# One transposition in place of two for the sinks' weights in a fused sink-attention and feed-forward kernel

## The chip, the cores and the metric

The kernel runs on one core of a Trainium2 chip. The metric is the device time of one execution in microseconds (us), as the median of three runs. One execution was taken by the hardware profiler; all rows below come from that one.

## The reference

Attention with a sliding window and sinks, then a feed-forward block on its output:

```python
B, H, S, D = 4, 8, 768, 64              # float32 all through
keep = (pos_k < n_sink) | ((rel >= 0) & (rel < window))     # n_sink 4, window 128
a = softmax(where(keep, q @ k.T / sqrt(D), -1e9))
x = (a @ v)  as [B*S = 3072, H*D = 512]
h = x @ w_in                            # 512 x 2048
g = h * erf(softplus(h))
out = g @ w_out                         # 2048 x 512
```

## The kernel before

**Steps and units.** The attention is cut into 48 steps. Step `s` takes 256 queries of two heads: `g, c = divmod(s, 4)` gives a block of 256 rows and a pair of heads; three blocks make one batch. The feed-forward block is cut into 192 units (12 row blocks of 256 by 16 slices of the hidden width), and four units go with one step. The position of a step on the planner's time axis is `pos(s)`, 54 for step 15 and four more for each next step; a unit is one position.

**A step's parts** have one-letter names in the plan: `q` and `v` load (SyncE's queue), `p` (`prep`) transposes q and k into the PSUM tile `tqk`, `s` (`score`) makes the scores `ps`, `f` (`soft`) masks them on VectorE and takes exponents on ScalarE into `pst`, `n` (`norm`) divides by the sums, `t` (`ptrans`) transposes the window's weights into `tp`, `w` (`sinkw`) and `u` (`strans`) deal with the sinks' weights, `a` (`av`) multiplies with v, `x` (`xfin`) splits the result into a high and a low part. `H`, `A`, `P` and `R` are the feed-forward block: first product, activation, second product and result. `k` (`sinks`) prepares the sinks' rows of v once per batch.

**The sinks' weights.** `pst` holds 144 columns for each of four quarters (two tiles of queries `i` by two heads `h`): 128 for the window and 16 for the sinks. `sinkw` splits the sinks' columns on VectorE into rounded, rest and rounded again (two copies and a subtraction into `sh`), `strans` transposes `sh` twice, once for each tile of queries, into the PSUM tile `ts`, and one ScalarE copy makes `sp` from it. `av` multiplies `sp` (128 rows: rounded, rest, rounded, zeros) by `sv`, whose rows are v's rounded part twice, v's rest, and zeros.

**Buffers.** `tqk`, `tp`, `ts` and `av` share the two PSUM buffers of the tag `t`. A buffer is free for the next tile when the last reader of its tile is done. `sp` has two buffers, `pst` a ring of two.

**What sets the order.** Every part is emitted with a priority worked out from its place on the time axis (`at`), and a planner orders each engine's instructions by its own costs and those priorities. The first steps follow lists written out by hand. From the position `fixed = pos(NF1) - 0.5` on, TensorE's instructions are chained in the order of the plan; VectorE, ScalarE and GpSimd stay with the planner. Between the lists and `fixed` the planner orders TensorE too. The plan's rows for a step differ on the two sides of `NF1`: in the free part the scores and `av` come at `a + 0.14`, the transpositions at `a + 2.15`; in the fixed part at `a - 0.3` and `a + 3.01`, with loads and `prep` earlier.

Of the kernel before, what the change touches and what calls it, by code (L numbers as in the profile page):

```python
# [9 lines left out]
F32 = mybir.dt.float32  # L10
BF16 = mybir.dt.bfloat16
F32R = mybir.dt.float32r
I32 = mybir.dt.int32
AF = mybir.ActivationFunctionType
ALU = mybir.AluOpType
# [4 lines left out]
P = 128  # L20
SW = 16
# [18 lines left out]
LO = 4.5  # L40

NE, AL = 4, 2
NF1 = 16

PW, EA = 256, 40
O = dict(prep=-100, norm=-100, core=-300, av=-300, load=-400, ptrans=-200, xfin=-100,
# [21 lines left out]
def kernel(  # L68
# [11 lines left out]
    nc = tc.nc  # L80
# [3 lines left out]
    NPAIR = H // 2  # L84
# [3 lines left out]
    GPB = S // GT  # L88
    NG = B * GPB
    NU = 4  # L90
    NSTEP = NG * NPAIR
    KB = P + SW
    scale = 1.0 / math.sqrt(D)
# [5 lines left out]
    ident = cpool.tile([P, P], F32, name="ident")  # L99
# [36 lines left out]
    def fast_path():  # L136
        with ExitStack() as st:
            pers = st.enter_context(tc.tile_pool(name="pers", bufs=1))
            raw = st.enter_context(tc.tile_pool(name="raw", bufs=2))
            qkp = st.enter_context(tc.tile_pool(name="qkp", bufs=1))  # L140
            work = st.enter_context(tc.tile_pool(name="work", bufs=2))
# [14 lines left out]
                out=kw[:, :256], in0=rf[:, :256], scalar=0.0, in1=kw[:, :256], op0=ALU.is_ge, op1=ALU.mult  # L156
# [28 lines left out]
            sv = pers.tile([P, NPAIR, P], F32R, name="sv")  # L185
            nc.gpsimd.memset(sv.bitcast(F32), 0.0)

            pst = pers.tile([P, RING, 2, 2, KB], F32, name="pst")

            shs = [pers.tile([P, 7, 2 * SW], F32R, name=f"sh{i}") for i in range(2)]  # L190
            for x in shs:
                nc.gpsimd.memset(x[:, 6].bitcast(F32), 0.0)
            pers.tile([P, 32], F32, name="gap")
            xp = {}

            stp, tail = {}, {}
# [44 lines left out]
            vec, ten, syn = (Line(x) for x in (nc.vector, nc.tensor, nc.sync))  # L241
# [25 lines left out]
            def sinks(s):  # L267

                g, c = divmod(s, NPAIR)
                d = stp[s]  # L270
                if g % GPB == 0:
                    for r0 in (0, 32):
                        (nc.gpsimd.tensor_copy if s < NE else nc.scalar.copy)(sv[r0 : r0 + 32, c, :], d["sv"])
                    vec.tensor_tensor(sv[64:96, c, :], d["sv"], sv[:32, c, :].bitcast(F32), op=ALU.subtract)

            dx = KB + 80
            X = [80, 80 + dx]
# [38 lines left out]
            def soft(s):  # L316
# [26 lines left out]
                if gb < GPB - 1:  # L343
                    syn.dma_start(kq[:, c, 0, :P], kq[:, c, 2, :P])

            def norm(s):
                d = stp[s]
                sm = d["sum"]
                vec.tensor_scalar_add(sm, sm, 1.0e-9)
                fill()  # L350
                vec.reciprocal(sm, sm)
                fill()
                for i in range(2):
                    for h in range(2):
                        p = d["pst"][:, i, h, :]
                        if 4 <= s < 8:
                            nc.scalar.activation(p, p, AF.Copy, scale=sm[:, i, h : h + 1])
                        else:
                            vec.tensor_scalar_mul(p, p, sm[:, i, h : h + 1])
# [20 lines left out]
            def sinkw(s):  # L380

                d = stp[s]
                sh = shs[s % 2][:, :6].rearrange("p (i r) t -> p i r t", i=2)
                x = d["pst"][:, :, :, P:]
                for r in (0, 2):
                    vec.tensor_copy(sh[:, :, r].rearrange("p i (h t) -> p i h t", h=2), x)
                vec.tensor_tensor(
                    sh[:, :, 1].rearrange("p i (h t) -> p i h t", h=2), x,
                    sh[:, :, 0].rearrange("p i (h t) -> p i h t", h=2).bitcast(F32), op=ALU.subtract,
                )  # L390
            def strans(s):

                d = stp[s]
                pool, tag = (ps_o, "o") if s < 6 else (ps_t, "t")
                ts = pool.tile([P, 2, P], F32, tag=tag, name=f"ts_{s}")
                for i in range(2):
                    x = shs[s % 2][:, 3 * i : 3 * i + 4].rearrange("p r t -> p (r t)").bitcast(F32)
                    ten.transpose(out=ts[:, i, :], in_=x, identity=ident)
                sp = d["sp"] = work.tile([P, 2, P], F32R, tag="sp", bufs=AL, name=f"sp_{s}")
                nc.scalar.copy(sp, ts)  # L400
# [44 lines left out]
            def pos(s):  # L445

                return 3 * s if s < NE else 4 * s - 4 * NE + 3 * NE - 2
# [34 lines left out]
            def fill():  # L482

                for w in list(todo):
                    try:
                        next(w)
                    except StopIteration:
                        todo.remove(w)
# [24 lines left out]
            def add(a, nm, j):  # L513
                ev.append((a, len(ev), nm, j))
# [23 lines left out]
            def use(n):  # L538
# [3 lines left out]
            order = sorted(range(32), key=use)  # L542
            acts = {
                "q": ("load", loadqk), "v": ("load", loadv), "p": ("prep", prep), "k": ("prep", sinks), "s": ("core", score),
                "f": ("core", soft), "n": ("norm", norm), "t": ("ptrans", ptrans), "w": ("ptrans", sinkw), "u": ("ptrans", strans),
                "a": ("av", av), "x": ("xfin", xfin), "H": ("hid", hid), "A": ("act", act), "P": ("proj", proj), "R": ("res", res),
                "L": ("wl", lambda j: wload(order[j])), "C": ("wc", lambda j: todo.append(wconv(order[j], j))), "D": ("wc", drain),
# [6 lines left out]
            def needs(nm, j):  # L554

                pin = [("C", order.index(n)) for n in range(j // NC * NC, j // NC * NC + NC)] if nm == "H" else []
                return {
                    "p": [("q", j), ("f", j - NPAIR)],
                    "s": [("p", j), ("f", j - 1 if j != 3 else 0)] if j > 1 else [("p", j)],
                    "f": [("s", j), ("t", j - (4 if j < 6 else 2)), ("w", j - (4 if j < 6 else 2))],  # L560
                    "n": [("f", j)],
                    "t": [("n", j), ("a", j - AL)],
                    "w": [("n", j), ("u", j - 2)],
                    "u": [("w", j), ("t", j)],
                    "k": [("v", j), ("p", j)],
                    "a": [("u", j), ("v", j)] + [("k", j)] * (j < NE),
                    "x": [("a", j)],
                    "H": pin + [("x", 3), ("f", 2), ("H", j - 1)] + [("A", j - 3)] * (j % 2 == 0),
                    "A": [("H", j), ("P", j - 4)],
                    "P": [("A", j | 1), ("C", order.index(16 + j if j < 16 else 0)), ("u", 5)],  # L570
                    "q": [("p", j - 2)],
                    "v": [("a", j - 3)],
                    "C": [("L", j)],
                    "L": [("C", j - WQ)],
                }.get(nm, [])
# [3 lines left out]
            done, a = set(), LEAD - 10  # L579
            while any(lines):  # L580
                before = len(done)
                for x in lines:
                    while x and all(w in done for w in needs(*x[0]) if w in known):
                        w = x.pop(0)
                        a = LEAD + w[1] if w[0] == "H" else a + 0.012
# [4 lines left out]

            fixed = pos(NF1) - 0.5
            for s in range(NE, NSTEP + AL):
                a = pos(s)
                if s < NF1:
                    plan = (
                        ("a", a + 0.139, s - AL), ("x", a + 1.11, s - AL), ("n", a + 1.12, s), ("p", a - 2.87, s), ("k", a - 2.869, s),
                        ("s", a + 0.14, s), ("f", a + 0.141, s), ("t", a + 2.15, s), ("w", a + 2.151, s), ("u", a + 2.152, s),
                        ("q", a - 3.84, s), ("v", a - 3.839, s),
                    )
                else:  # L600
                    plan = (
                        ("a", a - 0.3, s - AL), ("s", a - 0.29, s), ("f", a - 0.289, s), ("x", a - 0.285, s - AL), ("n", a + 1.12, s),
                        ("w", a + 2.151, s), ("t", a + 3.01, s), ("u", a + 3.02, s),
                        ("q", a - (8.2 if s > NF1 + 1 else 6.5 - 2 * (s - NF1)), s), ("p", a - (4.28 if s > NF1 else 2.87), s),
                        ("k", a - 2.869, s), ("v", a - 3.839, s),
                    )
                for nm, z, n in plan:
                    if NE <= n < NSTEP and (nm, n) not in done and (nm != "k" or n // NPAIR % GPB == 0):
                        add(max(z, last + 0.01) if nm in "ntwu" else z, nm, n)
            for m in range(NG * NF):  # L610
                g, f = divmod(m, NF)
                a = m + LEAD
                p = LAG + 0.3
                if a + p > fixed:
                    p = LAG + (1.0 if m % 2 == 0 else 0.0) + (0.01 if m % 4 > 1 else 0.03) + 0.005 * (m % 2)
# [80 lines left out]
    def general_path():  # L696

        NT_S = S // P
        with ExitStack() as st:
# [71 lines left out]
            with tc.tile_pool(name="g_one1", bufs=1) as one, tc.tile_pool(name="g_work1", bufs=2) as work:  # L771
# [3 lines left out]
                with tc.For_i(0, B, 1) as b:  # L775
                    for gb in range(GPB):
# [25 lines left out]
                        for i in range(2):  # L802
# [3 lines left out]
                            )  # L806

    fast_path()
    ok = nc.values_load(flagi[0:1, 0:1], min_val=0, max_val=1)
    with tc.If(ok == 0):  # L810
# [31 lines left out]
```

## Time and profile before

| | |
|---|---|
| median of three runs | 749.41 us (748.31 to 750.84) |
| the profiled execution | 750.56 us, of which the span from first to last instruction is 748.8 us |
| granted TensorE clock, mean | 0.994 |
| TensorE busy | 713.3 us, 95% of the span |
| VectorE busy | 506.2 us, 68% |
| ScalarE busy | 534.2 us, 71% |
| GpSimd busy | 185.7 us, 25% |

How to read it: PE is TensorE's matmul row, PEld its weight loads, DVE VectorE, ACT ScalarE, POOL GpSimd, SP SyncE. A busy time is the union of the instructions' recorded stretches; matmuls overlap each other in the record, so that the distance from one start to the next, and not the duration, says how much of TensorE one takes.

### The profile page before, as it was taken

What the parts mean: (1) busy time and instruction counts of PE and PEld (TensorE: products, weight loads), DVE (VectorE), ACT (ScalarE), POOL (GpSimd) and SP (SyncE); (2) the same over time, 40 slices, a digit from 0 to 9 for tenths busy, and PEclk for the clock granted to TensorE, in tenths of its full rate; (3) what the DMA queues carried; (4) which work ended last, traced back from release to release, by engine and by line L of the source; (5) the groups of instructions that cost most, each with busy time, mean ns of one, the idle gap of its engine ahead of it and who ended that gap; (6) DMA issues with size and microseconds to landing.
All of it is one profiled execution on the core that took longest, in us unless ns stands there. A gap on an engine that the chain in (4) does not pass through costs nothing. (4 is left out here: it accounts for less than half of the span.)

```text
span 748.8 us, 14851 instructions
## 1 busy us (share of the span) xinstructions
PE 713.3 (95%) x5168; PEld 593.3 (79%) x5168; DVE 506.2 (68%) x1493; ACT 534.2 (71%) x1265; POOL 185.7 (25%) x220
## 2 busy tenths in 40 slices
PE   4888999899999999999999999999999999999996
PEld 2564666677788888888888888888888888888995
DVE  7899999897776566576566666556667566563442
ACT  3576769776786867778677777777787776775663
POOL 2220001222322322332232232232232232232221
PEclk9899999999999999999999999999999999999999
DMA  5687541111121121111111211112112211000000
GB/s 143 186 251 273 200 148 43 34 29 37 54 58 29 57 54 26 54 34 40 54 44 43 57 39 41 54 24 50 46 38 54 61 29 36 29 13 1 29 1 32
DMA packets 100595, 47.33 MB, mean 63 GB/s; under 512 B 89248, under 2 KB 93344, under 8 KB 100512
## 3 DMA queue, kind: packets, MB, share of 16 engines
q1 hardware_dynamic: 99680, 46.16, 22.0%
q8 instruction: 43, 0.70, 0.4%
q14 instruction: 40, 0.33, 0.1%
q10 hardware_dynamic: 832, 0.13, 0.1%
HBM read 37.88 MB, written 6.29 MB: 59 GB/s over the span
## 5 line engine op out<-in xcount | busy, mean ns | idle before, releaser
L234 PE MATMUL o<-wt,g 128*128 128x512 f32 x1056 | 261.3, 395 | 1.7 <-POOL g L674 0.8
L234 PEld LDWEIGHTS o<-wt,g 128*128 128x128 f32 x1056 | 191.4, 188 | 39.4 <-POOL g L674 1.7
L674 POOL TENSOR_TENSOR g<-acc,g 128x512 fp32r<-128x512 f32 x88 | 116.1, 1319 | 335.4 <-DVE g L234 321.8
L234 PE MATMUL h<-xh,wt 128*128 128x256 f32 x1408 | 195.0, 281 | 2.5 <-DVE acc L234 2.4
L234 PEld LDWEIGHTS h<-xh,wt 128*128 128x128 f32 x1408 | 178.1, 188 | 10.1 <-DVE acc L234 3.5
L665 ACT ACTIVATE u<-r 128x512 f32<-128x512 f32 x288 | 163.3, 623 | 13.8 <-DVE acc L234 8.5
L234 DVE SCALAR_TENSOR_TENSOR acc<-u,h 128x512 f32<-128x512 f32 x88 | 60.4, 687 | 133.8 <-ACT u L665 70.9
L234 DVE SCALAR_TENSOR_TENSOR acc<-u,acc 128x512 f32<-128x512 f32 x176 | 122.6, 697 | 22.8 <-ACT u L665 7.7
L340 ACT ACTIVATE pst<-pst,kq 128x144 f32<-128x144 f32 x192 | 77.6, 406 | 56.7 <-DVE kq L234 56.4
L234 PE MATMUL h<-xl,wt 128*128 128x256 f32 x704 | 109.9, 277 | 0.0
L375 POOL TENSOR_SCALAR_AFFINE_SELECT uo<-pt 128x512 f32<-128x512 f32 (+1 forms) x96 | 62.8, 676 | 188.6 <-ACT pt L371 188.6
L234 PEld LDWEIGHTS h<-xl,wt 128*128 128x128 f32 x704 | 93.3, 188 | 0.3 <-DVE wf L234 0.2
L660 ACT ACTIVATE r<-h 128x512 f32<-128x512 f32 x96 | 56.8, 591 | 49.2 <-PE h L234 48.9
L662 ACT ACTIVATE r<-r 128x512 f32<-128x512 f32 x96 | 61.2, 638 | 2.0
L661 ACT ACTIVATE r<-r 128x512 f32<-128x512 f32 x96 | 61.1, 636 | 2.1
L234 PE MATMUL ps<-kq 64*64 64x208 f32 (+1 forms) x768 | 50.5, 374 | 6.1 <-ACT kq L262 4.6
L262 ACT COPY kq<-tqk 128x512 f32<-128x512 f32 x48 | 28.0, 583 | 34.5 <-PE tqk L234 34.5
L234 PE MATMUL av<-uo,v 128*64 128x128 f32 (+1 forms) x512 | 49.8, 327 | 0.0
L234 DVE CUSTOM_DVE_ANT_0 pst<-ps,mask 128x144 f32<-128x144 f32 x192 | 47.6, 304 | 1.6
L234 DVE COPY_PREDICATED ps<-tri,ps 64x256 f32<-64x256 int8 (+1 forms) x100 | 41.6, 420 | 4.8 <-PE ps L234 1.7
L234 DVE CAST g<-acc 128x512 fp32r<-128x512 f32 x88 | 40.0, 454 | 6.1 <-PE tp L234 0.9
L234 PEld LDWEIGHTS ps<-kq 64*64 64x64 f32 x768 | 27.9, 139 | 20.2 <-issue 9.8
(77 smaller groups left out, 689.6 us busy)
## 6 DMA issues: line engine op xcount, KB each, us to landing
ws<-in_moe_w_in_dram SPq DMA_DIRECT2D x16, 512.0 KB, 4.6
ws<-in_moe_w_out_dram SPq DMA_DIRECT2D x16, 512.0 KB, 6.8
v<-in_v_dram SPq DMA_DIRECT2D x64, 96.0 KB, 2.4
out_dram<-ot SPq DMA_DIRECT2D x24, 256.0 KB, 2.2
q<-in_q_dram SPq DMA_DIRECT2D x95, 64.0 KB, 2.2
k<-in_k_dram SPq DMA_DIRECT2D x95, 64.0 KB, 2.2
v<-in_v_dram SPq DMA_DIRECT2D x32, 64.0 KB, 2.2
kq<-kq SPq DMA_DIRECT2D x32, 64.0 KB, 2.2
```

The costliest lines, as they stand in the source:

```text
L234: ins = f(*a, **k)
L262: nc.scalar.copy(kq[:, c, 1:, :P], tp)
L340: nc.scalar.activation(y, y, AF.Exp, bias=d["neg"][:, i, h : h + 1], scale=-1.0, accum_out=d["sum"][:, i, h : h + 1])
L375: nc.gpsimd.affine_select(out=uo[:, :, i1:, e, :], in_=pt[:, :, i1:, :], pattern=[[0, 2], [0, 2 - i1], [-sg, P]], compare_op=op, fill=0.0, ...
L660: nc.scalar.activation(r, h, AF.Tanh, bias=b_t, scale=0.5)
L661: nc.scalar.activation(r, r, AF.Square, bias=b_v, scale=-0.5)
L662: nc.scalar.activation(r, r, AF.Square, bias=b_r)
L665: nc.scalar.activation(u, r, AF.Square, bias=b_a[i], scale=CS)
L674: nc.gpsimd.tensor_tensor(gl, acc, gh.bitcast(F32), op=ALU.subtract)
```

## The change

From step 9 (`NW`) on, `norm` writes the sinks' columns, already divided, into a tile of 128 columns that holds the 64 columns of both query tiles twice (`both`), and divides only the 128 window columns in `pst`. `strans` transposes that tile once. ScalarE reads `ts` twice, each time with a per-partition factor of ones and zeros (`own`) that keeps the rows of one query tile, and rounds into `sp`. `sinkw` comes behind it and fills the rests: for each query tile, VectorE subtracts 32 rounded rows in `sp` from the same rows of `ts` and writes them to another 32 rows of `sp`. The rest of v's rows is then wanted twice, and GpSimd copies it into `sv[96:]` once for each pair and batch from step 9 on. `NF1` goes from 16 to 15: step 15 is planned as the later ones were, and TensorE's fixed order begins at the position 53.5, not 57.5. The loads and `prep` of steps 15 to 17 get other places on the axis with it.

```diff
-NF1 = 16
+NW = 9
+NF1 = 15
...
-            pers.tile([P, 32], F32, name="gap")
+            own = pers.tile([P, 32], F32, name="gap")[:, :2]
+            nc.gpsimd.memset(own, 0.0)
+            for i in range(4):
+                nc.gpsimd.memset(own[32 * i : 32 * i + 32, i % 2 : i % 2 + 1], 1.0)
...
+                if s >= NW and (g % GPB == 0 or s < NW + NPAIR):
+                    nc.gpsimd.tensor_copy(sv[96:, c, :], sv[64:96, c, :])
...
+            def both(s):
+                return shs[s % 2].rearrange("p r t -> p (r t)")[:, :P].bitcast(F32)
...
+                if s >= NW:
+                    x, y = (
+                        t.rearrange("p (o n) t -> p o n t", o=1).broadcast_to([P, 2, 4, SW])
+                        for t in (
+                            d["pst"].rearrange("p i h t -> p (i h) t")[:, :, P:],
+                            sm.rearrange("p i (h o) -> p (i h) o", o=1).broadcast_to([P, 4, SW]),
+                        )
+                    )
+                    vec.tensor_tensor(both(s).rearrange("p (r n t) -> p r n t", r=2, n=4), x, y, op=ALU.mult)
...
-                        p = d["pst"][:, i, h, :]
+                        p = d["pst"][:, i, h, : P if s >= NW else KB]
...
+                if s >= NW:
+                    ts, sp = d["ts"], d["sp"]
+                    for i in range(2):
+                        r, t = (slice(32 * x, 32 * x + 32) for x in (i, 1 - i))
+                        vec.tensor_tensor(sp[t, i, :], ts[r], sp[r, i, :].bitcast(F32), op=ALU.subtract)
+                    return
...
+                if s >= NW:
+                    ts = d["ts"] = pool.tile([P, P], F32, tag=tag, name=f"ts_{s}")
+                    ten.transpose(out=ts, in_=both(s), identity=ident)
+                    sp = d["sp"] = work.tile([P, 2, P], F32R, tag="sp", bufs=AL, name=f"sp_{s}")
+                    for i in range(2):
+                        nc.scalar.activation(sp[:, i, :], ts, AF.Copy, scale=own[:, i : i + 1])
+                    return
...
-                    "w": [("n", j), ("u", j - 2)],
-                    "u": [("w", j), ("t", j)],
+                    "w": [("n", j), ("u", j - 2)] if j < NW else [("u", j)],
+                    "u": [("w" if j < NW else "n", j), ("t", j)],
...
-                    "a": [("u", j), ("v", j)] + [("k", j)] * (j < NE),
+                    "a": [("u", j), ("w", j), ("v", j)] + [("k", j)] * (j < NE),
...
-                        ("s", a + 0.14, s), ("f", a + 0.141, s), ("t", a + 2.15, s), ("w", a + 2.151, s), ("u", a + 2.152, s),
+                        ("s", a + 0.14, s), ("f", a + 0.141, s), ("t", a + 2.15, s), ("w", a + (2.151 if s < NW else 2.153), s), ("u", a + 2.152, s),
...
-                        ("w", a + 2.151, s), ("t", a + 3.01, s), ("u", a + 3.02, s),
+                        ("t", a + 3.01, s), ("u", a + 3.02, s), ("w", a + 3.021, s),
...
-                    if NE <= n < NSTEP and (nm, n) not in done and (nm != "k" or n // NPAIR % GPB == 0):
+                    if NE <= n < NSTEP and (nm, n) not in done and (nm != "k" or n // NPAIR % GPB == 0 or NW <= n < NW + NPAIR):
```

## Rows read from the trace of the kernel before

**Rows 1.** The page, busy time of each engine
```profile
PE 713.3 (95%) x5168; PEld 593.3 (79%) x5168; DVE 506.2 (68%) x1493; ACT 534.2 (71%) x1265; POOL 185.7 (25%) x220
```
**Rows 2.** Busy time by stretch: length, engines' us (instructions), granted clock, DMA share, GB/s
```profile
110.00:150.00 40.00, 36.99 (x258) 27.08 (x257) 35.95 (x87) 33.68 (x75) 7.96 (x8) 1.00 0.16 41
150.00:205.00 55.00, 50.64 (x363) 41.16 (x361) 44.25 (x123) 40.71 (x103) 14.47 (x18) 1.00 0.16 40
205.00:738.00 533.00, 533.00 (x4041) 463.77 (x4038) 325.48 (x981) 391.49 (x905) 143.19 (x152) 1.00 0.15 39
```
**Rows 3.** TensorE's waits, 110 to 205 us: us in total, times, longest
```profile
PE h L234 <- DVE acc L234: 2.4, 5, 0.7
PE tp L234 <- DVE pst L234: 2.1, 3, 1.5
PE ts L234 <- DVE sh L234: 1.9, 4, 0.6
PE o L234 <- POOL g L674: 0.8, 2, 0.5
```
**Rows 4.** TensorE's timeline over a step of the fixed order: start, length
```profile
399.73 0.60 PE L234 MATMUL tp<-ident,pst 128*128 128x128 f32 x4
400.17 0.38 PE L234 MATMUL ts<-ident,sh 128*128 128x128 f32 x2
400.31 3.00 PE L234 MATMUL o<-wt,g 128*128 128x512 f32 x12
...
405.07 0.44 PE L234 MATMUL tqk<-ident,k 128*128 128x128 f32 x2
...
413.79 0.38 PE L234 MATMUL tp<-ident,pst 128*128 128x128 f32 x2
```
**Rows 5.** The tile ts on TensorE: times each, shortest, median and longest ns
```profile
L234 PE MATMUL ts<-ident,sh x96: 271/273/477, 17.8 to 670.1; 128*128 128x128 f32 x96
```
**Rows 6.** The tile ts by stretch: PE, PEld, ACT
```profile
205.00:749.00 544.00, 12.59 (x66) 8.35 (x66) 12.35 (x33) 1.00 0.15 39
```
**Rows 7.** VectorE's timeline, norm and sinkw of one step
```profile
409.62 0.91 DVE L234 TENSOR_SCALAR pst<-pst,kq 128x144 f32<-128x144 f32 x4
410.57 0.30 DVE L234 CAST sh<-pst 128x64 fp32r<-128x64 f32 x2
410.80 0.23 DVE L234 TENSOR_TENSOR sh<-pst,sh 128x64 fp32r<-128x64 f32 x1
```
**Rows 8.** ScalarE's timeline behind the transpositions of rows 4
```profile
401.48 0.37 ACT L400 CAST sp<-ts 128x256 fp32r<-128x256 f32 x1
...
402.42 1.67 ACT L665 ACTIVATE u<-r 128x512 f32<-128x512 f32 x3
```
**Rows 9.** VectorE's timeline in the same stretch
```profile
403.14 0.69 DVE L234 SCALAR_TENSOR_TENSOR acc<-u,h 128x512 f32<-128x512 f32 x1 [1.55 <-ACT u L665]
...
405.01 0.68 DVE L234 SCALAR_TENSOR_TENSOR acc<-u,acc 128x512 f32<-128x512 f32 x1
```
**Rows 10.** Groups by shape: times each, busy us, mean ns of one, idle before
```profile
L234 DVE TENSOR_TENSOR xl<-av,xh 128x256 fp32r<-128x256 f32 x44 | 18.4, 418 | 1.1 <-ACT xh L437 0.9
...
L357 ACT ACTIVATE pst<-pst,kq 128x144 f32<-128x144 f32 x16 | 5.3, 407 | 0.6 <-DVE kq L234 0.6
...
L273 POOL CAST sv<-v 32x128 fp32r<-32x128 f32 x8 | 3.2, 404 | 15.8 <-DMA v<-in_v_dram 15.5
...
L163 DVE TENSOR_TENSOR kw<-kw 128x128 f32<-128x128 f32 x1 | 0.3, 270 | 0.0
```
**Rows 11.** TensorE's timeline, a step of the free part
```profile
144.93 0.44 PE L234 MATMUL ts<-ident,sh 128*128 128x128 f32 x2 [0.61 <-DVE sh L234]
...
147.35 0.44 PE L234 MATMUL tqk<-ident,k 128*128 128x128 f32 x2
```
**Rows 12.** SyncE's queue: issues of the loads of q and k
```profile
208.01 0.37 SPq L234 DMA_DIRECT2D k<-in_k_dram  x1
```
**Rows 13.** TensorE's timeline, its first instructions
```profile
4.10 0.66 PE L234 MATMUL tqk<-ident,k 128*128 128x128 f32 x2 [4.10 <-DMA k<-in_k_dram]
```

## The prediction

> **What bounds the kernel now.** I read the page first: TensorE is busy for 95% of the span, the others for 25 to 71% [rows 1]. A mean over stages decides nothing, so next comes the busy time by stretch [rows 2]. From 205 us to 738 us TensorE is busy for 533.00 of 533.00 us at a granted clock of 1.00, its 2.4 GHz level, while VectorE is busy for 61% and ScalarE for 73% of that stretch: here only work taken from TensorE's own stream shortens anything. From 110 to 205 us, where steps 9 to 14 run, TensorE is busy for 87.6 of 95 us, and VectorE for 35.95 of 40 us in the first part: nobody is the bound alone. The waits of that stretch say what TensorE stands still for: nearly all of it is VectorE, 2.4 us for the activation's first product, 2.1 us for `pst` (norm) and 1.9 us for `sh` (sinkw), and 0.8 us for GpSimd [rows 3]. Last I read one step of the fixed order instruction by instruction [rows 4]: from one `tp` to the next it lasts 413.79 - 399.73 = 14.06 us without a pause.
>
> **TensorE.** The change takes one transposition of two from each step from 9 on, 39 of the 48. 66 records of `ts` lie behind 205 us, two for each of steps 15 to 47 [rows 6]: 33 of the 39 go where TensorE is the bound, 6 in the mixed stretch. One transposition's price is read from starts: four `tp` move the next start by 400.17 - 399.73 = 0.44 us, 0.11 each; the two `ts` move the first second-product matmul by 400.31 - 400.17 = 0.14 us, 0.07 each [rows 4]. I take 0.11, since the instruction that remains still pays whatever the passage to another kind costs, and keep 0.07 as the lower end. Behind 205 us: 33 x 0.11 = 3.6 us (lower end 2.3). Ahead of it: 6 x 0.11 = 0.65 us.
>
> The record of one transposition is 273 ns long [rows 5]. The Trainium skill, "TensorE: Matmul & The Clock Gate", Part 4: PE-mode transpose, gives about 275 ns for one in a kernel's context, and 39 of those would be an estimated 10.7 us. The record agrees with that length, but not that it is what TensorE loses: the starts are 0.11 us apart. As a rival it is taken up below.
>
> **VectorE, norm and sinkw.** Gone per step: the split into `sh`, 410.57 to 411.03, 0.46 us [rows 7], and 16 of 144 columns in four multiplications that take 410.57 - 409.62 = 0.95 us (a tenth at most, 0.1). New: one product of 128x128, at most 0.27 us by the nearest row, and two subtractions of 32x128 out of PSUM, for which the nearest row is 0.42 us at twice the columns: between 0.21 and 0.42 each [rows 10]. Sum between +0.1 and +0.6 us a step; I take +0.2, by half the columns. Behind 205 us it costs nothing: VectorE idles 39% there, `pst` is done at about 410.6 and its transposition starts at 413.79, so 0.2 us of delay falls into 3.2 us [rows 4, 7]. Ahead of 205 us `tp` does wait for `pst`: the product stands in front of the multiplications, 0.27 - 0.1, about 0.15 us later in up to four steps, 0.6 us lost. In return `sh` no longer comes behind `pst` with a low priority; it is written before it. The 1.9 us in which `ts` waited for `sh` go [rows 3]. VectorE is nearly full in part of that stretch, and the wait for the next product stands right behind, so I count half, 0.95 us.
>
> **ScalarE and the longer chain behind `ts`.** One copy of 0.37 us [rows 8] becomes two of half the columns with a per-partition factor. A copy with such a factor on 144 columns takes 0.41 us [rows 10]: the pair costs between 0.37 and 0.81 us, +0.44 at most; ScalarE's 27% of idle time behind 205 us is 3.8 us a step. The PSUM buffer of `ts` is now freed by the last VectorE subtraction, not by ScalarE's copy. Who is queued behind it: `tqk` of the step after next at 405.07, which takes that buffer in the tag's turn of two [rows 4]. ScalarE's first half can run where the copy runs now, at 401.48, the second in the gap ahead of 402.42 or inside it [rows 8], ending by 402.7 with the upper price; VectorE stands idle for 1.55 us until 403.14 [rows 9], so the subtractions end at 403.1, or one activation product later, 403.9 and 0.4 for each of them. Both are before 405.07. `av` reads `sp` a whole step later. Cost nothing, cover 1 to 2 us.
>
> **GpSimd and the start.** 15 copies of 32x128 at 0.40 us [rows 10] (steps 9 to 15, 24 to 27, 36 to 39), each wanted by an `av` more than a step later, on an engine idle for 75%: nothing. Were one late by its own length, 15 x 0.4 = 6 us is the upper end; no `av` follows so close. Five memsets for `own` stand in the program behind the identity matrix, and the first transposition waits until 4.10 for a load [rows 13]: nothing.
>
> **The fixed order from 53.5.** Step 15 gets the places of later steps: `av` and scores 0.43 of a position (1.5 us) earlier, the transpositions 0.86 later, `prep` of step 16 at -4.28 and not -2.87. TensorE's work is the same, and step 15 lies wholly behind 205 us, where no idle time is left to win [rows 2]. Moved with it are the four loads of q and k for steps 15 to 17 on SyncE's queue, past those of v, the output and the shifted keys. What sets them is the pair of buffers, not the plan: the load at 208.01 [rows 12] follows `tqk` of step 16 and serves step 18, two periods of 14 us on. Cost nothing; were they late in full, one landing once.
>
> **The sum** against the profiled execution: 750.56 - 3.6 - 0.65 - 0.95 + 0.6 = 746.0 us. That execution lies 1.15 us above the median of its three; the same change on the median is 749.41 - 4.6 = 744.8 us. **Predicted: 744.8 us.**
>
> **Rivals.**
> *The mixed stretch gives it back.* For it: VectorE is 90% busy up to 150 us, gets up to 0.6 us more a step, and `tqk` comes only 147.35 - 144.93 = 2.4 us behind `ts` there [rows 11], with the subtractions in a full queue. Against it: if `sh` is early, `ts` can follow `tp` and the distance grows. Price: 6 x 0.4 us, and the 1.9 us not won; 3.6 - 2.4 = 1.2 us of gain remain: 748.2 us on the median.
> *`tqk` waits for the subtractions (slower).* The planner may put them behind the third activation product of rows 9, which ends at 405.01 + 0.68 = 405.69. Two subtractions of 0.25 us then free the buffer at 406.2, 1.1 us after 405.07, in each of 33 steps: 36 us lost, 4.6 won, 781 us. It decides from the point where the buffer comes free 0.11 us behind 405.07. Beside it: "Trainium Kernel Development and Optimization" of the Trainium skill, Best Practices, says that consistent bubbles can mean that PSUM ran out; no row of before shows one behind 205 us. Against it: `w`'s place on the axis is ahead of `xfin` and the next `soft`, and VectorE is idle when its input comes.
> *The whole record falls out.* 39 x 0.273 = 10.6 us, 738.8 us on the median. The skill's figure named above would give the same. Against it: two starts 0.11 us apart [rows 4].
>
> **How the numbers follow.** A measurement of this kernel tells about 0.3%, 2.25 us, from no change. Forecast 0.74, gain between 2.3 and 7 us (lower: 0.07 each; upper: 3.6 + 0.65 + all of the 1.9 us + 1.5 of the other 5.3 us of rows 3, less 0.6): faster. Given back 0.14: within. Slower 0.09, whole record 0.03, faster. Together 0.77, 0.14 and 0.09. The range holds the forecast's ends and half of the second case, and leaves out the stall and the whole record: 742.3 to 748.0 us.
>
> **What would show it.** Right: 57 records of `ts` in place of 96, periods near 14.06 - 0.11 = 13.95 us (and 0.11 less where a step is longer), no TensorE wait behind 205 us, the `ts` waits before it gone. Wrong: a wait of `tqk` for VectorE's writing of `sp`, new idle time between 110 and 205 us that passes 2 us, or steps behind 205 us that are not shorter by 0.1 us.

## The result, and the profile after

The changed kernel takes 743.23 us (median of four runs, 742.50 to 744.02) against 749.91 us before (also four runs): ratio 0.9906, 95% interval 0.9893 to 0.9920. A second series gave 743.75 us and 0.9921 (0.9908 to 0.9935). So 5 to 8 us are won; 4.6 us were forecast, 744.8 us, with a range of 742.3 to 748.0 us. The profiled execution took 743.36 us with a span of 741.7 us.

The page, busy time of each engine; it answers to [rows 1]:
```profile
PE 708.9 (96%) x5129; PEld 590.3 (80%) x5129; DVE 513.7 (69%) x1493; ACT 543.0 (73%) x1304; POOL 193.4 (26%) x240
```
TensorE has 39 instructions fewer, ScalarE 39 more and 8.8 us more work, VectorE as many as before and 7.5 us more work, GpSimd 7.7 us more. The tile `ts` on TensorE, against [rows 5]:
```profile
L238 PE MATMUL ts<-ident,sh x57: 272/273/477, 17.9 to 663.4; 128*128 128x128 f32 x57
```
57 records stand where 96 stood, of the same length. Busy time by stretch, as in [rows 2]:
```profile
110.00:150.00 40.00, 37.18 (x262) 27.95 (x261) 35.70 (x83) 34.13 (x78) 7.83 (x8) 1.00 0.18 45
150.00:205.00 55.00, 51.33 (x384) 41.80 (x383) 47.50 (x128) 43.69 (x111) 17.85 (x23) 1.00 0.16 41
205.00:731.00 526.00, 526.00 (x3974) 457.57 (x3973) 329.13 (x977) 396.71 (x934) 144.75 (x159) 1.00 0.15 39
```
The picture is the old one: TensorE without a pause behind 205 us, VectorE nearly full up to 150 us. TensorE's waits between 110 and 205 us, against [rows 3]:
```profile
PE tp L238 <- ACT wt L528: 2.8, 3, 1.2
PE h L238 <- DVE acc L238: 2.1, 5, 0.6
PE av L238 <- ACT pt L389: 1.1, 1, 1.1
PE o L238 <- POOL g L705: 0.3, 1, 0.3
```
The wait of `ts` for `sh` is gone. That of `tp` has grown from 2.1 to 2.8 us (the view names ScalarE's `wt`, a copy of weights, but VectorE is in the division of `pst` at that moment), and `av` waits 1.1 us for ScalarE's copy of `tp`, which is new; 7.2 us have become 6.3 us. In a second trace of the kernel before (e11 below) the four waits of [rows 3] come to 5.9 us, 1.3 of them for `sh`: that the waits fell in sum is not shown. A step of the fixed order, as in [rows 4], on TensorE's timeline:
```profile
395.12 0.60 PE L238 MATMUL tp<-ident,pst 128*128 128x128 f32 x4
395.55 0.27 PE L238 MATMUL ts<-ident,sh 128*128 128x128 f32 x1
395.58 3.00 PE L238 MATMUL o<-wt,g 128*128 128x512 f32 x12
...
400.35 0.44 PE L238 MATMUL tqk<-ident,k 128*128 128x128 f32 x2
...
409.07 0.60 PE L238 MATMUL tp<-ident,pst 128*128 128x128 f32 x4
```
One transposition stands where two stood, and the step lasts 409.07 - 395.12 = 13.95 us, where it lasted 14.06. ScalarE behind it, against [rows 8]:
```profile
395.87 0.58 ACT L389 COPY pt<-tp 128x512 f32<-128x512 f32 x1
396.33 0.64 ACT L424 ACTIVATE sp<-ts,gap 128x128 fp32r<-128x128 f32 x2
```
And VectorE, against [rows 9]:
```profile
396.75 0.43 DVE L238 CAST g<-acc 128x512 fp32r<-128x512 f32 x1
397.21 0.58 DVE L238 TENSOR_TENSOR sp<-ts,sp 32x128 fp32r<-32x128 f32 x2
398.91 0.69 DVE L238 SCALAR_TENSOR_TENSOR acc<-u,h 128x512 f32<-128x512 f32 x1 [1.13 <-POOL g L705]
```
The pair of factors takes 0.64 us, the pair of subtractions 0.58 us, and they end at 397.79, 2.56 us ahead of `tqk`. It is not so everywhere. In step 38, on VectorE and on TensorE:
```profile
540.02 0.28 DVE L238 TENSOR_TENSOR sp<-ts,sp 32x128 fp32r<-32x128 f32 x1
540.33 0.82 DVE L238 CAST g<-acc 128x512 fp32r<-128x512 f32 x1
541.18 0.28 DVE L238 TENSOR_TENSOR sp<-ts,sp 32x128 fp32r<-32x128 f32 x1
```
```profile
541.66 0.44 PE L238 MATMUL tqk<-ident,k 128*128 128x128 f32 x2
```
There 0.2 us are left, the least of all steps (0.9 us in the second trace, e5): the rival of a late `tqk` did not come, but it was near.

**Where the time went.** Three marks stand in every trace: the first score matmul of step 9, of step 17 and of step 47. In the changed kernel:
```profile
112.41 0.99 PE L238 MATMUL ps<-kq 64*64 64x208 f32 x16
...
230.23 0.99 PE L238 MATMUL ps<-kq 64*64 64x208 f32 x16
...
653.68 0.99 PE L238 MATMUL ps<-kq 64*64 64x208 f32 x16
```
From the first to the second (eight steps) 117.82 us, from the second to the score of step 47 (thirty steps) 423.45 us. Before, the same marks are (the view's window cuts the sixteen matmuls to fourteen):
```profile
112.85 0.92 PE L234 MATMUL ps<-kq 64*64 64x208 f32 x14
...
233.46 0.92 PE L234 MATMUL ps<-kq 64*64 64x208 f32 x14
...
660.31 0.92 PE L234 MATMUL ps<-kq 64*64 64x208 f32 x14
```
Between them lie 120.61 and 426.85 us. So 3.4 us were won in the thirty steps, 0.113 us in each, and 2.8 us in the eight ahead of them, where the prediction had 1.2 us (1.0 ahead of step 15 and two steps at 0.11). What is left of the 7.1 us between the two spans lies ahead of step 9 (0.44 us) and behind the mark of step 47 (0.53 us); two traces of one kernel differ by 0.5 to 0.7 us ahead of step 9 (the table below), and by about 0.2 us behind step 47.

The eight steps hold the same matmuls in both kernels but for the transpositions, so their time can be split into TensorE's pauses and the rest, in which the view has TensorE busy. Length of the eight steps and TensorE's busy time in the kernel before, in the changed one and in e3 (below, with two transpositions again):
```profile
112.85:233.46 120.61, 113.24 (x819) 90.67 (x818) 96.69 (x260) 94.41 (x225) 31.01 (x34) 1.00 0.16 40
...
112.41:230.23 117.82, 111.33 (x812) 89.91 (x811) 98.38 (x259) 95.46 (x233) 33.16 (x38) 1.00 0.16 41
...
112.20:231.69 119.49, 111.73 (x819) 90.46 (x819) 98.56 (x259) 95.42 (x233) 33.19 (x38) 1.00 0.16 40
```
The pauses are 7.4 us before (7.0 us in e2, 6.0 us in e11) and 6.5 us after (6.3 us in e5). The busy part fell by 1.9 us (by 1.5 us against e2's 112.86), of which eight transpositions at 0.107 us are 0.9 us; in e3, with as many transpositions as before, it is still 1.5 us lower (1.1 us against e2). So a good part of what was won here is neither fewer transpositions nor a wait that the views list: the same matmuls, in another order, follow each other more closely.

### The profile page after: what moved, and what is told of

Read it like the earlier page. It is cut to its first block, busy times and chain, and to the rows that moved or that the text cites. A ratio compares the mean times of both kernels' runs of the same rounds, so it can differ in the third digit from the quotient of the medians.

```text
span 741.7 us, 14935 instructions
## 1 busy us (share of the span) xinstructions
PE 708.9 (96%) x5129; PEld 590.3 (80%) x5129; DVE 513.7 (69%) x1493; ACT 543.0 (73%) x1304; POOL 193.4 (26%) x240
## 5 line engine op out<-in xcount | busy, mean ns | idle before, releaser
L393 POOL TENSOR_SCALAR_AFFINE_SELECT uo<-pt 128x512 f32<-128x512 f32 (+1 forms) x96 | 64.7, 694 | 195.5 <-ACT pt L389 175.8
L238 DVE SCALAR_TENSOR_TENSOR wf<-ws,wf 128x512 int32<-128x512 int32 x64 | 44.2, 728 | 0.4
```

The lines of the kernel that those rows point to most:

```text
L238: ins = f(*a, **k)
L393: nc.gpsimd.affine_select(out=uo[:, :, i1:, e, :], in_=pt[:, :, i1:, :], pattern=[[0, 2], [0, 2 - i1], [-sg, P]], compare_op=op, fill=0.0, ...
```

## The experiments

All starts are read from TensorE's timeline as above; "7" is from the scores of step 9 to those of step 16, "8" to those of step 17, "30" from step 17 to step 47, in us.

| run | ratio to before (95%) | start of step 9 | 7 | 8 | 30 |
|---|---|---|---|---|---|
| before | | 112.85 | 106.55 | 120.61 | 426.85 |
| before again (e11) | single run | 112.11 | 105.51 | 119.57 | 426.65 |
| changed | 0.9906 (0.9893 to 0.9920) | 112.41 | 103.86 | 117.82 | 423.45 |
| changed again (e5) | 0.9921 (0.9908 to 0.9935) | 112.90 | 103.68 | 117.64 | 423.44 |
| e1, changed, NF1 16 | 0.9959 (0.9945 to 0.9973) | 112.85 | 105.75 | 119.70 | 423.44 |
| e2, before, NF1 15 | 1.0006 (0.9998 to 1.0015) | 112.47 | 105.77 | 119.83 | 426.72 |
| e3, two transpositions | 1.0001 (0.9988 to 1.0013) | 112.20 | 105.43 | 119.49 | 426.64 |
| e4, new way from step 15 | 0.9948 (0.9933 to 0.9962) | 112.45 | 105.42 | 119.38 | 423.43 |
| e7, changed, NF1 14 | 0.9935 (0.9920 to 0.9949) | 112.72 | 104.65 | 118.59 | 423.44 |
| e8, changed, NF1 13 | 0.9940 (0.9925 to 0.9955) | 112.93 | 105.21 | 119.16 | 423.44 |
| e9, before, early split | 1.0010 (1.0001 to 1.0019) | 113.02 | 107.06 | 121.12 | 427.11 |
| e10, changed, later `t` | 0.9911 (0.9896 to 0.9925) | 112.54 | 103.00 | 116.95 | 423.44 |
| e12, no subtractions | 0.9964 (0.9949 to 0.9978) | 112.93 | 105.34 | 119.29 | 423.75 |

**e11, how far a trace repeats.**

> The kernel before once more, one look, for a second trace of the stretch from step 9 to step 17: within 0.5 us of 120.6 us. Only if it is, differences of 1 us and more between the traces of different kernels in that stretch can be read as the kernels'.

The thirty steps repeat within 0.2 us, the eight only within 1.04 us: the expectation missed. Between two kernels, a difference of 1 us in "8" says little; the changed kernel's two traces agree within 0.2 us and lie 1.8 to 3.0 us below the two of before.

**e3, TensorE's part alone.**

```diff
-ts = d["ts"] = pool.tile([P, P], F32, tag=tag, name=f"ts_{s}")
-ten.transpose(out=ts, in_=both(s), identity=ident)
+ts = d["ts"] = pool.tile([P, 2, P], F32, tag=tag, name=f"ts_{s}")
+for i in range(2):
+    ten.transpose(out=ts[:, i, :], in_=both(s), identity=ident)
...
-    nc.scalar.activation(sp[:, i, :], ts, AF.Copy, scale=own[:, i : i + 1])
+    nc.scalar.activation(sp[:, i, :], ts[:, i, :], AF.Copy, scale=own[:, i : i + 1])
```
(and `ts[r, i, :]` in the subtractions)

> The changed kernel, but the tile of doubled columns is transposed twice, into two halves of ts that hold the same, from step 9 on; ScalarE and VectorE do what they do in the change. It puts back TensorE's 39 transpositions alone. By starts (0.11 us each): 4.3 us slower than the changed kernel, ratio to before 0.996, periods 14.06 and 14.28 us. By the length of the record (0.273 us each): 10.6 us slower, ratio 1.005. If the gain came from the chain on the other engines and not from TensorE: as fast as the changed kernel, 0.991.

The run took 749.20 us, as long as before, 5.5 to 6 us above the changed kernel. By the time all three expectations missed: the price by starts gave 4.3 us and 0.996. The periods came as that price had them, 14.06 and 14.28 us: the thirty steps cost 426.64 - 423.44 = 3.20 us more, 0.107 each: the distance of the starts, not the length of the record. In the eight steps one new pause shows, more than TensorE's work. ScalarE stood in front of the exponents for a late load of v's sink rows, and `tp` of step 14 paid for it; ScalarE's and TensorE's timelines of this run:
```profile
195.64 0.62 ACT L277 CAST sv<-v 32x128 fp32r<-32x128 f32 x2 [1.83 <-DMA v<-in_v_dram]
```
```profile
199.07 0.30 PE L238 MATMUL tp<-ident,pst 128*128 128x128 f32 x1 [1.78 <-ACT ot L725]
```
Without these 1.78 us the eight steps would, by subtraction, be at 117.7 us, the changed kernel's time with eight more transpositions in them. Up to that pause the two kernels run alike: step 14's scores start 78.72 us behind step 9's here, and 78.67 and 78.48 us in the two traces of the changed kernel.

**e1, e2, e4: what the earlier fixed order is worth.** e1 sets `NF1 = 16` in the changed kernel, e2 sets `NF1 = 15` in the kernel before, e4 sets `NW = 15` in the changed one.

> The changed kernel with NF1 back at 16: one transposition, old begin of the fixed order. Theory A (what was won ahead of step 16, 2.7 us of the trace between the scores of step 9 and of step 16, comes with the one transposition and with the sinks' columns being ready early): ratio to before 0.990 to 0.992, and these seven steps within 0.7 us of the 103.9 us of the changed kernel. Theory B (it comes with the earlier fixed order): ratio 0.993 to 0.995, the seven steps at 105.5 us or more. Behind step 16 both expect periods of 13.95 and 14.17 us.

> The kernel before with NF1 at 15 and nothing else. Theory A: ratio 0.999 to 1.002, seven steps from step 9 at 106 to 107 us. Theory B: ratio 0.996 to 0.998, the seven steps at 104.5 to 105.5 us. Periods behind step 16 unchanged at 14.06 and 14.28 us by both.

> The changed kernel with the new way from step 15 on, not from step 9: 33 steps, all of them where TensorE is never idle. NF1 is 15. Theory A: 33 x 0.11 = 3.6 us of gain and nothing ahead of it, ratio 0.995, seven steps from step 9 at 106 us or a little over. Theory B: these 3.6 us and most of 1.9 us ahead of it, ratio 0.9925 to 0.9935, seven steps at 104.5 us or less.

e2 says that NF1 alone wins nothing (theory A), e1 that without it the new way loses 1.9 to 2.1 us of the trace (theory B's seven steps; its ratio, 0.9959, is past theory B's range too). Both theories took the edits for a sum, and they are none. e1 shows the place, at the border between the planner's order and the fixed one, on TensorE's timeline:
```profile
210.18 4.97 PE L238 MATMUL o<-wt,g 128*128 128x512 f32 x21
214.99 0.27 PE L238 MATMUL tp<-ident,pst 128*128 128x128 f32 x1
215.10 0.27 PE L238 MATMUL ts<-ident,sh 128*128 128x128 f32 x1
215.21 0.49 PE L238 MATMUL tp<-ident,pst 128*128 128x128 f32 x3
217.48 0.39 PE L238 MATMUL av<-sp,sv 128*128 128x256 f32 x1 [1.78 <-ACT pt L389]
```
The planner puts all second products ready, 21 matmuls, ahead of the transpositions of step 15; nothing is left between `tp` and the `av` that opens the fixed order. `av`, which shares the tag's two PSUM buffers with `tp`, waits 1.78 us for ScalarE's copy of it. In the fixed order twelve matmuls, 2.8 us, stand there. e4 wins 3.9 us, by 33 transpositions at 0.107 us 3.5 us; its eight steps, at 119.38 us, are those of before: theory A's gain (its seven steps, 105.42 us, lie under theory A's 106, but the kernel before has 105.51 us itself in e11).

**e7 and e8: the border elsewhere.** `NF1 = 14` and `NF1 = 13` in the changed kernel.

> The changed kernel with the fixed order from step 14 on (NF1 14). Theory A: NF1 is worth only the pause that the planner's order leaves at its border, 1.78 us in the run with 16; with 14 the border moves one step ahead and the result is the changed kernel's within 1.5 us. Theory B: each step that goes from the planner's order to the fixed one wins 1 us or more, ratio 0.988 or lower.

> The changed kernel with the fixed order from step 13 on (NF1 13). Theory A: VectorE still has the weights' conversion there, so the fixed order waits for it: slower than the changed kernel by up to 3 us. Theory B: ratio 0.987 or lower.

Both are slower than with 15, by 1.2 and 1.9 us in the median of their runs against e5 and by 0.8 to 1.5 us in "8" of their traces, and both have at the border what e1 has: their timelines show `av` behind `tp` waiting for ScalarE's copy, 0.74 us at 187.77 and 1.25 us at 173.38. Theory A held for 14; for 13 it held in size, not in the cause that it named, and the granted clock fell behind that pause (last section). With 15 the border falls where matmuls stand between.

**e9 and e12: is it VectorE?** e9 moves only the old split, in the kernel before:
```diff
-("w", a + 2.151, s)
+("w", a + (2.151 if s < 9 else 1.121), s)
```


> The kernel before with one number of the plan changed: from step 9 on, sinkw is placed right behind norm in the free part and not behind ptrans, so that sh is split before VectorE goes on. Two transpositions, old split, NF1 16. Theory A (what the change won ahead of step 15, beyond TensorE's work, is that ts no longer waits for sh): the 1.9 us of ts waits go, ratio 0.997 to 0.9985, periods from step 9 on like the changed kernel's 16.2 and 13.5 us. Theory B (another wait for VectorE takes their place at once): ratio 0.999 to 1.002, periods as before, 18.2 and 15.4 us.

The ratio is 1.0010: no gain. TensorE's waits of this run, 110 to 215 us:
```profile
PE h L234 <- DVE acc L234: 3.9, 5, 2.1
PE tp L234 <- DVE pst L234: 2.8, 3, 1.5
PE ts L234 <- DVE sh L234: 0.3, 2, 0.2
```
`ts` waits 0.3 us and not 1.9, and the other two waits for VectorE have grown by 1.5 and 0.7 us [rows 3]; all waits come to 7.0 us, where they came to 7.2. Theory B is right in size; the order of the steps is new, though, as the periods are neither the old ones nor those expected. e12 takes the two subtractions out of the changed kernel (`sinkw` returns at once):

> The changed kernel without the two subtractions behind ts: the rests of the sinks' weights stay zero, so that their small part of the result is left out. VectorE has 0.58 us less a step, and the buffer of ts is free with ScalarE's second copy. If VectorE's work sets the pace from step 9 to 14, 6 x 0.58 = 3.5 us go there: eight steps from step 9 at 114.5 us, ratio 0.987. If its queue is only one of several that are late by turns: less than 1 us, eight steps at 117 us or more, ratio 0.990 to 0.993. Behind step 17 both expect periods of 13.95 and 14.17 us, as VectorE has time to spare there.

With 0.58 us less on VectorE in each step the eight steps take 119.29 us, 1.5 us more, and the median of the runs is 2.2 to 2.7 us above the changed kernel's. Neither theory: less work is slower. Its first periods are 18.0, 9.1 and 18.7 us, near e9's 18.3, 9.3 and 18.7 and far from the changed kernel's 16.2, 13.5 and 17.0: the planner had ordered the stretch anew. The granted clock fell in both traces as well (last section), so how much of the 1.5 us is the order and how much the clock stays open.

**e10: the transpositions later in the free part.**
```diff
-("t", a + 2.15, s), ("w", a + (2.151 if s < NW else 2.153), s), ("u", a + 2.152, s),
+("t", a + (2.15 if s < NW else 2.6), s), ("w", a + (2.151 if s < NW else 2.603), s), ("u", a + (2.152 if s < NW else 2.602), s),
```


> The changed kernel with the transpositions, strans and sinkw placed 0.45 of a position later in the free part from step 9 on. In the changed kernel tp still waits 2.8 us for pst ahead of step 15, in three steps. If that is the planner taking pst for ready too early, matmuls that it puts in between hide it: up to 2.5 us faster than the changed kernel, ratio 0.988 to 0.990. If VectorE's queue is what is late, the waits move to the activation's product: within 1 us of the changed kernel.

`tp` waits 1.4 us and not 2.8, the eight steps take 116.95 us, 0.7 to 0.9 us less; the time, 742.54 us, cannot be told from the changed kernel's. That is the second expectation's time, but not its reason: the activation's product waits less too (1.3 us and not 2.1), and it is `av` that waits longer, 1.6 us and not 1.1.

**e5, the changed kernel again.**

> The changed kernel once more, for a second trace beside those of the other runs. Ratio 0.990 to 0.993, TensorE's seven steps from step 9 within 0.3 us of 103.86 us; what differs between its two traces lies ahead of step 9 and behind the last matmul.

As expected: 743.75 us, seven steps at 103.68 us.

**e6: the price of a late buffer.** Each subtraction eight times over:
```diff
-vec.tensor_tensor(sp[t, i, :], ts[r], sp[r, i, :].bitcast(F32), op=ALU.subtract)
+for _ in range(8):
+    vec.tensor_tensor(sp[t, i, :], ts[r], sp[r, i, :].bitcast(F32), op=ALU.subtract)
```


> The changed kernel with each of the two subtractions behind ts done eight times over, with the same result: 14 more in a chain, 0.29 us each, 4.1 us a step. Theory A, the price of the rival that the prediction named: tqk waits for the buffer of ts once the subtractions end later than it may start. In most steps of the changed kernel they end 2.98 us ahead of it, so that 1.1 us a step is lost: 30 to 40 us, 773 to 785 us, with tqk waiting in nearly every step. Theory B (the buffer isn't what tqk waits for, or the planner takes another one): no wait of tqk, under 5 us lost.

It took 834.57 us, ratio 1.1137 (1.1119 to 1.1154), far more than either theory gave. TensorE's waits from 205 us on:
```profile
PE tqk L238 <- DVE xl L238: 38.9, 28, 2.2
PE tqk L238 <- issue: 11.6, 3, 4.5
PE h L238 <- DVE acc L238: 2.8, 2, 2.5
```
`tqk` does wait, 1.1 to 1.3 us in an ordinary step, but for VectorE's `xl`, which frees the buffer of `av`. The subtractions end later still, so `tqk` must have been given the other buffer of the two: theory A's size in such a step, theory B's way. Three steps wait up to 4.5 us, and a third of the loss lies ahead of step 17 (147.2 us there, against 117.8).

## Why the prediction was right, and where it was not

**One transposition is worth 0.11 us, not 0.27: shown.** The thirty steps give 0.113 and 0.107 us by the two traces of before against those of the change, and e3 gives 0.107 with nothing else changed. For 33 steps that is 3.5 to 3.7 us, where 3.6 were forecast. The rival of the whole record is out, and so is the figure of the Trainium skill as a price ("TensorE: Matmul & The Clock Gate", Part 4: PE-mode transpose, about 275 ns): the record is still 273 ns long, near the skill's figure, but what falls out of a full stream is the distance of the starts.

**No cost behind 205 us: right, with less cover than was said.** TensorE's list of waits stays empty there. The pair of factors took 0.64 us (bounds 0.37 to 0.81), a subtraction 0.28 (0.21 to 0.42), and `ts` is free 2.6 us ahead of `tqk` in the step shown, where 1 to 2 us were forecast, but 0.2 us in step 38. The rival's price, 1.1 us a step, is near what e6 measured in an ordinary step, but by chance: there `tqk` waits for the buffer of `av`, so that it keeps to the buffer of `ts` when that one is late was wrong.

**0.65 us for six transpositions ahead of step 15: not shown.** e3 puts the work back, and steps 9 to 13 take as long. TensorE pauses there anyhow.

**Half of the 1.9 us in which `ts` waits for `sh`, less 0.6 us for a later `tp`: not borne out.** `tp` did wait longer (2.6 and 2.8 us in two traces, 2.1 and 1.7 before), as forecast. But e9 takes the same wait away by itself and wins nothing, and the pauses of the eight steps, 6.5 and 6.3 us, lie among those of the old way (7.4 us before, 7.0 in e2, 6.0 in e11, where the clock had fallen). The mean of all and nothing was a guess about a queue that the planner lays out anew.

**"The fixed order from 53.5 ... cost nothing": the step that failed.** It was costed against the order of before, where the border shows no pause; there e2 agrees (1.0006). In the changed kernel the planner arrives at the border with another order, and NF1 16 leaves 1.78 us of pause in e1. Of the 1.8 to 3.0 us won from step 9 to step 17, that much hangs on it.

**What stays open** is why the planner's order for the new way is the shorter one. Cut at the score of step 14, the eight steps fall into two parts. The first lasts 79.90, 78.83, 79.24 and 78.98 us in four traces with the old way there (before twice, e2, e4) and 78.67, 78.48, 78.52 and 78.72 us in four with the new one (changed twice, e1, e3), with two or three matmuls of the second product more done in it. The second lasts 40.4 to 40.7 us with the old, 39.15 and 39.17 us in the changed kernel. No single term accounts for that: e9 and e12, with less waiting for `sh` or less work, were laid out in slower orders, and e3 without its late load would be as fast with all its transpositions. That the forecast for this stretch, 1.2 us, has the right sign is no proof of its terms, and that the whole came within the range is in part luck: the term behind 205 us is right, while the eight steps gave 2.8 us for 1.2 us, by an order that the prediction had not costed.

## What to carry to other kernels

Where an engine is busy without a pause, price an instruction by how far it moves the next start, and that price holds to a few per cent. Where a planner lays out the order, an edit is not a sum of its parts: it can draw a new order for a whole stretch, and the kernel with less work can be the slower one, as e12 was. There, split the time into pauses and busy time before a gain is put down to a wait. Look at the border between a free and a fixed order for what stands between a transposition and the next taker of its buffer.

## What the runs showed of the hardware

The granted clock fell for some microseconds behind a pause of TensorE in e4, e8, e9, e10, e11 and e12, and several times in e6; in the other traces, both of the changed kernel among them, it stayed at 1.00 from 112 to 236 us. In e12, where `tp` waited 1.73 us at 136.96:
```profile
138.00:142.00 4.00, 3.92 (x30) 2.30 (x31) 3.90 (x5) 2.46 (x6) 3.41 (x4) 0.60 0.14 32
```
A mean of 0.60 over 4 us means that TensorE stood at its 1.2 GHz level for most of it. The sixteen score matmuls in that stretch of e9, which has the same dip (0.67), took 1.77 us, and 0.99 us at the full level.

The length of the pause alone does not decide it. In the two traces of the kernel before, `tp` waited 1.46 us (up to 136.80) and 1.47 us (up to 135.99) in the same step, and TensorE was busy for 2.27 of 4 us around both pauses; behind the first the clock stayed, behind the second it fell:
```profile
134.00:138.00 4.00, 2.27 (x11) 1.39 (x9) 2.86 (x10) 2.67 (x11) 0.00 (x0) 1.00 0.21 48
138.00:142.00 4.00, 3.85 (x28) 3.34 (x28) 3.93 (x5) 2.62 (x5) 3.23 (x3) 1.00 0.00 0
```
```profile
134.00:138.00 4.00, 2.27 (x13) 1.53 (x12) 2.82 (x10) 2.67 (x10) 0.40 (x1) 0.95 0.09 21
138.00:142.00 4.00, 4.00 (x22) 3.96 (x22) 3.96 (x5) 1.36 (x4) 2.98 (x3) 0.62 0.00 0
```
Nor does the dip by itself set the time of the eight steps: e11 has it and takes 119.57 us, 1.04 us less than the trace without it, and e10 has it and is the fastest of all, at 116.95 us. How much of what e8, e9 and e12 lost is the clock's is not shown.
